# The last block's stores cut at multiples of 16 rows and dealt to three DMA queues, its second half stored first

## Chip, cores, metric

One NeuronCore of a Trainium2 chip runs the whole program. The metric is the device time of an execution in microseconds (us); lower is better. Before the change: 2807.3 us, median of three executions.

## The reference, cut to what matters

```python
def reference(**kwargs):
    X = np.fft.rfft(x, axis=1)                       # x: (8, 3008, 256)
    y = np.fft.irfft(X * (filt_r + 1j * filt_i)[None], n=3008, axis=1)
    x = y.reshape(8 * 3008, 256)
    h = x @ w_in                                     # (24064, 2048)
    g = h * np.clip(h + 3.0, 0.0, 6.0) / 6.0
    return g @ w_out                                 # (24064, 256), float32
```

## The kernel before

The filter is done by small DFT matmuls beside the two large matrix products. The products go over 47 blocks of 512 tokens, each in eight steps (376 steps). When a block's last matmul is done, DVE puts its output tile `o` together from PSUM, Pool adds a part that ACT has copied to the tile `p`, and SP stores it. (The engines: PE does the matmuls, DVE, ACT and Pool work on elements, and SP, ACT and Pool can each issue DMAs; what one of them issues is called its queue here. A DMA has landed at its last semaphore event in the trace. DRAIN is an instruction that every engine has in the program's closing line.) For all blocks but the last that happens beside the next block's matmuls. The last block has nothing beside it.

```python
N, NA, NC, TOK, BLK, P, D = 3008, 47, 64, 94, 512, 128, 256

def out_4(k):
    p5 = st["po", k][2][:, 0, :, :]
    nc.vector.tensor_tensor(out=o_at(k, 1, 1), in0=p5, in1=o_at(k, 1, 0), op=ALU.add)                     # L493
    nc.vector.tensor_tensor(out=o_at(k, 0, 1), in0=p5, in1=o_at(k, 0, 1), op=ALU.add)                     # L494
    nc.gpsimd.tensor_tensor(out=o_at(k, 1, 0), in0=st["o", k][1][:, 1, :, :], in1=o_at(k, 1, 0), op=ALU.add)  # L495

def out_5(k):
    nc.vector.tensor_tensor(out=o_at(k, 0, 1), in0=st.pop(("po", k))[3][:, 1, :, :], in1=o_at(k, 0, 1), op=ALU.add)  # L498
    o = st.pop(("o", k))[0].rearrange("p t u d -> p (t u) d")
    t, end = k * BLK, (k + 1) * BLK
    while t < end:
        b, r = divmod(t, N); j, r = divmod(r, TOK); h, a = divmod(r, NA)   # (written on one line here)
        p = t % P
        m = min(NA - a, P - p)
        nc.sync.dma_start(raw(out, b * N + a * NC + outer(j, h), [[NC * D, m], [1, D]]), o[p:p + m, t % BLK // P, :])  # L508
        t += m
# ... at the very end of the program:
out_4(NBLK - 1)
out_5(NBLK - 1)
```

Tokens lie in runs of 47 whose rows are 64 rows apart in the output, so one store carries at most 47 rows of 1 KB. Pool also issues DMAs of its own all through the body: 224 stores of `z_tmp`, 84 of `g_tmp` and 16 loads of weights, 324 in all, the last at 2196.5 us.

Of the kernel before, what the change touches and what calls it, by code (L numbers as in the profile page):

```python
# [13 lines left out]
ALU = mybir.AluOpType  # L14
# [8 lines left out]
N = 3008  # L23
NA = 47
NC = 64
KH = 24
NF = N // 2 + 1
P = 128
D = 256
# [14 lines left out]
BLK = 512  # L44
NBLK = B * N // BLK
# [4 lines left out]
def outer(j, h):  # L50

    return (NC - j if j else HC) if h else j
# [49 lines left out]
def kernel(  # L102
# [9 lines left out]
    nc = tc.nc  # L112
# [11 lines left out]
    def pool(name, bufs, **kw):  # L124
        return ctx.enter_context(tc.tile_pool(name=name, bufs=bufs, **kw))
# [13 lines left out]
    op = pool("op", 2)  # L139
# [16 lines left out]
    st = {}  # L156

    def raw(src, row, ap):
        return bass.AP(tensor=src.tensor, offset=src.offset + row * D, ap=ap)
# [184 lines left out]
    for b in range(B):  # L344
        j = 0
# [5 lines left out]
    def token(i):  # L351
        b, j, n = chunks[i]
        return b * N + j * TOK, n * TOK
# [124 lines left out]
    def o_at(k, t, d):  # L478
        return st["o", k][0][:, t, :, ts(d, P)]
# [11 lines left out]
# [5 lines that stand above are left out]

    def out_5(k):
        nc.vector.tensor_tensor(out=o_at(k, 0, 1), in0=st.pop(("po", k))[3][:, 1, :, :], in1=o_at(k, 0, 1), op=ALU.add)  # L498
        o = st.pop(("o", k))[0].rearrange("p t u d -> p (t u) d")

        t, end = k * BLK, (k + 1) * BLK
        while t < end:
            b, r = divmod(t, N)
            j, r = divmod(r, TOK)
            h, a = divmod(r, NA)
            p = t % P
            m = min(NA - a, P - p)
            nc.sync.dma_start(raw(out, b * N + a * NC + outer(j, h), [[NC * D, m], [1, D]]),  # L508
                              o[p:p + m, t % BLK // P, :])
            t += m  # L510

# [9 lines left out]
    with tc.manual_schedule():  # L521
# [77 lines left out]
        for i in range(2, len(chunks)):  # L599
            k = token(i)[0] // BLK  # L600
# [52 lines left out]
        for i in range(len(items) + 1):  # L653
            up = i < len(items)
            k, p = items[min(i, len(items) - 1)]
            dn = i > 0
            kd, pd = items[i - 1]
            def do(early):
                for fn, a in plan.get((i, early), ()):
                    fn(*a)  # L660
# [23 lines left out]
            if dn and pd == 0 and kd:  # L684
                out_5(kd - 1)
# [8 lines left out]
                if pd == NP - 1:  # L694
                    out_3(kd)
            do(False)
        out_4(NBLK - 1)
        out_5(NBLK - 1)


# [28 lines left out]
```

## Time and profile before

| | before |
|---|---|
| time, median of 3 | 2807.3 us (2805.96 to 2807.75) |
| span of the profiled execution | 2805.7 us, granted clock 0.987 |
| end of the last matmul | 2785.3 us |
| first store of the last block issued | 2787.0 us |
| tail: end of the last matmul to end of span | 20.4 us |
| Pool's closing DRAIN | 2786.3 to 2795.6 us |

The **tail** is the number to watch: only this part of the program differs between the two kernels. On each engine the instructions before it are the same and in the same order. Its pieces are in the lines that the prediction shows.

### The profile page before, as it was taken

How to read it: one execution, taken by the hardware profiler on the slowest of the kernel's cores; microseconds unless marked ns; L12 is line 12 of the kernel's file. 1: busy time of each engine (PE TensorE's matmuls, PEld its weight loads, DVE VectorE, ACT ScalarE, POOL GpSimd, SP SyncE). 2: the span in 40 equal slices, each digit the busy share in tenths (PEclk: the TensorE clock that was granted, in tenths of full speed). 3: DMA queues.
4: the chain of work that ended last, by engine and by line, in shares of the span. 5: the costliest groups of instructions: out<-in, count | busy, mean ns of one | idle time of the engine just before them, and what ended most of it. 6: DMA issues, size and time to landing. Idle time of an engine off the chain costs nothing.

```text
span 2805.7 us, 47214 instructions
## 1 busy us (share of the span) xinstructions
PE 2700.1 (96%) x18096; PEld 2395.8 (85%) x18096; DVE 1993.9 (71%) x3463; ACT 1325.9 (47%) x2672; POOL 456.4 (16%) x663
## 2 busy tenths in 40 slices
PE   3589999999999999999999999999999999999997
PEld 1269888989889998899988998899988999999996
DVE  5877875777657776577756777567775777766665
ACT  1144445454554445544455445544455444445443
POOL 6470112110120111201021101210012100000000
PEclk9699999999999999999999999999999999999998
DMA  7544223321223212222133221332123321100000
GB/s 216 175 112 118 63 55 90 90 68 43 74 72 85 80 50 71 80 73 75 51 84 89 72 56 45 86 91 70 49 56 90 97 66 42 42 25 23 17 8 16
DMA packets 121800, 200.82 MB, mean 72 GB/s; under 512 B 22280, under 2 KB 86600, under 8 KB 121448
## 3 DMA queue, kind: packets, MB, share of 16 engines
q1 hardware_dynamic: 97108, 139.48, 17.3%
q0 software_dynamic: 19776, 52.46, 8.0%
q10 hardware_dynamic: 4692, 5.88, 0.7%
q8 instruction: 143, 2.34, 0.3%
q14 instruction: 81, 0.66, 0.1%
HBM read 122.75 MB, written 74.97 MB: 70 GB/s over the span
## 4 chain that ended last, share of the span: by engine, by line
PE 92%; DVE 3%; DMA 2%; ACT 1%; issue 1%; POOL 0%; SPq 0%; ACTq 0%; POOLq 0%; DVEq 0%
PE po L468 41%; PE al L392 23%; PE be L392 17%; PE psn L367 4%; PE psf L300 3%; PE psf L275 2%; PE psf L329 2%; DMA z_tmp<-t 1%; DVE g L442 0%; DVE y L319 0%; DMA g_tmp<-t 0%; DMA xn<-in_x_dram 0%; DVE s L314 0%; DVE s L313 0%; ACT t L278 0%
## 5 line engine op out<-in xcount | busy, mean ns | idle before, releaser
L468 PEld LDWEIGHTS po<-w_out,g 128*128 128x128 f32 x10528 | 1398.3, 192 | 152.4 <-issue 37.3
L468 PE MATMUL po<-w_out,g 128*128 128x128 f32 x10528 | 1430.6, 276 | 4.9 <-DVE g L442 4.6
L442 DVE SCALAR_TENSOR_TENSOR g<-r,h 128x512 f32<-128x512 f32 x752 | 519.0, 690 | 268.9 <-ACT r L437 256.1
L437 ACT ACTIVATE r<-h,half_c 128x512 f32<-128x512 f32 x752 | 542.7, 722 | 337.3 <-DVE h L418 325.1
L392 PE MATMUL al<-xt,w_in 128*128 128x256 f32 x2256 | 675.6, 381 | 6.4 <-DVE h L423 3.3
L418 DVE TENSOR_TENSOR h<-be,s 128x512 f32<-128x512 f32 x376 | 259.8, 691 | 272.1 <-PE be L392 250.5
L392 PE MATMUL be<-xn,w_in 128*128 128x256 f32 x1504 | 447.8, 379 | 0.0
L392 PEld LDWEIGHTS al<-xt,w_in 128*128 128x128 f32 x2256 | 342.6, 192 | 10.5 <-DVE h L423 3.8
L392 PEld LDWEIGHTS be<-xn,w_in 128*128 128x128 f32 x1504 | 286.1, 190 | 38.9
L432 ACT ACTIVATE h<-al 128x256 f32<-128x256 f32 x376 | 144.4, 384 | 355.6 <-PE al L392 355.6
L423 DVE TENSOR_TENSOR h<-al,s 128x256 f32<-128x256 f32 x376 | 159.6, 425 | 167.5 <-PE al L392 166.0
L450 DVE TENSOR_TENSOR g<-g 128x512 f32<-128x512 f32 x376 | 260.2, 692 | 12.9
L413 ACT ACTIVATE s<-al 128x256 f32<-128x256 f32 x376 | 144.6, 384 | 199.4 <-PE al L392 199.4
L404 ACT ACTIVATE s<-be 128x256 f32<-128x256 f32 x376 | 144.4, 384 | 181.0 <-PE be L392 181.0
L392 PE MATMUL al<-xn,w_in 128*128 128x256 f32 x752 | 225.2, 381 | 0.5 <-ACT h L432 0.5
L392 PE MATMUL be<-xt,w_in 128*128 128x256 f32 x752 | 224.1, 380 | 0.0
L288 POOL DMA_DIRECT2D z_tmp<-t x224 | 131.5, 591 | 417.2 <-ACT t L278 407.7
L452 DVE TENSOR_TENSOR g<-g 128x256 f32<-128x256 f32 x376 | 168.8, 449 | 12.8
L403 ACT ACTIVATE s<-al 128x256 f32<-128x256 f32 x376 | 144.5, 384 | 70.2 <-PE al L392 70.2
L495 POOL TENSOR_TENSOR o<-p,o 128x256 f32<-128x256 f32 x47 | 34.1, 725 | 878.1 <-ACT t L332 361.3
L449 DVE TENSOR_TENSOR g<-g 128x256 f32<-128x256 f32 x376 | 161.9, 430 | 12.8
L392 PEld LDWEIGHTS be<-xt,w_in 128*128 128x128 f32 x752 | 143.2, 190 | 19.4
(71 smaller groups left out, 1783.7 us busy)
## 6 DMA issues: line engine op xcount, KB each, us to landing
t<-z_tmp SPq DMA_DIRECT2D x48, 512.0 KB
t<-g_tmp SPq DMA_DIRECT2D x188, 120.0 KB
z_tmp<-t POOLq DMA_DIRECT2D x224, 96.0 KB, 3.0
g_tmp<-t POOLq DMA_DIRECT2D x84, 256.0 KB, 3.8
out_dram<-o SPq DMA_DIRECT2D x328, 47.0 KB
xs<-in_x_dram SPq DMA_DIRECT2D x120, 128.0 KB
ft<-in_filt_r_dram SPq DMA_DIRECT2D x96, 128.0 KB
ft<-in_filt_i_dram SPq DMA_DIRECT2D x96, 128.0 KB
```

The lines of the kernel that those rows point to most:

```text
L392: nc.tensor.matmul(ps, w_in[p][:, w, :], x, start=start, stop=stop, skip_group_check=True)
L403: nc.scalar.activation(out=s[:, 0, :], in_=al, func=AXT.Copy)
L404: nc.scalar.activation(out=s5, in_=be[:, 1, :], func=AXT.Copy)
L413: nc.scalar.activation(out=s[:, 1, :], in_=al, func=AXT.Copy)
L418: nc.vector.tensor_tensor(out=st["h"][0].rearrange("p (a n) -> p a n", a=2), in0=be, in1=s, op=ALU.add)
L423: nc.vector.tensor_tensor(out=st["h"][1][:, 256:512], in0=al, in1=s5, op=ALU.add)
L437: nc.scalar.activation(out=r, in_=st["h"][i], func=AXT.Relu, bias=half_c, scale=1.0 / 6.0)
L442: nc.vector.scalar_tensor_tensor(out=st["g", k, p][:, o:o + 2, :].rearrange("p a n -> p (a n)"), in0=st["r", i], scalar=1.0, in1=st["h"][i ...
L449: v.tensor_tensor(out=g[:, G1, :], in0=g[:, G3, :], in1=g[:, G22, :], op=ALU.add)
L450: v.tensor_tensor(out=g[:, G3:G2 + 1:2, :], in0=g[:, G3:G1 + 1, :], in1=g[:, G11:G11 + 1, :].broadcast_to([P, 2, 256]), op=ALU.subtract)
L452: v.tensor_tensor(out=g[:, G4, :], in0=g[:, G12, :], in1=g[:, G2, :], op=ALU.subtract)
L468: nc.tensor.matmul(st["po", k][bank][:, part, u, :], g[:, a, ts(u, P)], w_out[p][:, w, :], start=(p == 0 and n in OPENS and u == 0), stop= ...
```

## The change

Its intent: the stores of 47 rows run on one DMA engine, so cut the last block's stores into pieces whose row count many engines divide; deal them to SP, ACT and Pool in turn; and finish and store the second half of the block first, so that its stores go out while DVE still works on the first half. To do so, Pool's addition of the last block moves to DVE.

```diff
     def out_5(k):
         nc.vector.tensor_tensor(out=o_at(k, 0, 1), in0=st.pop(("po", k))[3][:, 1, :, :], in1=o_at(k, 0, 1), op=ALU.add)
-        o = st.pop(("o", k))[0].rearrange("p t u d -> p (t u) d")
-        t, end = k * BLK, (k + 1) * BLK
+        store(k, 0, 4)
+
+    def store(k, u0, u1, qs=None):
+        o = st["o", k][0].rearrange("p t u d -> p (t u) d")
+        t, end, i = k * BLK + u0 * P, k * BLK + u1 * P, 0
         while t < end:
...
             m = min(NA - a, P - p)
-            nc.sync.dma_start(raw(out, ...), o[p:p + m, t % BLK // P, :])
+            if qs:
+                m = m // 16 * 16 or m
+            q = qs[i % len(qs)] if qs else nc.sync
+            i += 1
+            q.dma_start(raw(out, ...), o[p:p + m, t % BLK // P, :])
             t += m
...
-        out_4(NBLK - 1)
-        out_5(NBLK - 1)
+        k, v, add = NBLK - 1, nc.vector.tensor_tensor, ALU.add
+        po, qs = st["po", k], (nc.sync, nc.scalar, nc.gpsimd)
+        v(out=o_at(k, 1, 1), in0=po[2][:, 0, :, :], in1=o_at(k, 1, 0), op=add)              # L708
+        v(out=o_at(k, 1, 0), in0=st["o", k][1][:, 1, :, :], in1=o_at(k, 1, 0), op=add)      # L709
+        store(k, 2, 4, qs)
+        v(out=o_at(k, 0, 1), in0=po[2][:, 0, :, :], in1=o_at(k, 0, 1), op=add)              # L711
+        v(out=o_at(k, 0, 1), in0=po[3][:, 1, :, :], in1=o_at(k, 0, 1), op=add)              # L712
+        store(k, 0, 2, qs)
```

More of the change, by code (lines that the diff above doesn't have):

```diff
@@ L507, in out_5 @@
             m = min(NA - a, P - p)
-            nc.sync.dma_start(raw(out, b * N + a * NC + outer(j, h), [[NC * D, m], [1, D]]),
+            if qs:
+                m = m // 16 * 16 or m
+            q = qs[i % len(qs)] if qs else nc.sync
+            i += 1
+            q.dma_start(raw(out, b * N + a * NC + outer(j, h), [[NC * D, m], [1, D]]),
                               o[p:p + m, t % BLK // P, :])
```

## The prediction

> **What bounds the kernel now.** I read the page first, for the bound of the body. Over 2780 of the 2806 us TensorE sets the pace, and the change leaves those instructions alone. The busy line and the first lines of the costliest groups say so; the reader should note that PE is at 96% of the span and that its idle time is a few us.
>
> ```profile
> PE 2700.1 (96%) x18096; PEld 2395.8 (85%) x18096; DVE 1993.9 (71%) x3463; ACT 1325.9 (47%) x2672; POOL 456.4 (16%) x663
> L468 PE MATMUL po<-w_out,g 128*128 128x128 f32 x10528 | 1430.6, 276 | 4.9 <-DVE g L442 4.6
> ```
>
> The change touches only what follows the last matmul, so I read the timeline from there. Columns are start, duration, engine, line, operation.
>
> ```profile
> 2782.33 2.94 PE L468 MATMUL po<-w_out,g 128*128 128x128 f32 x24 [0.62 <-DVE g L442]
> ...
> 2785.31 0.43 DVE L489 TENSOR_TENSOR o<-po,o 128x256 f32<-128x256 f32 x1
> 2785.77 0.42 DVE L493 TENSOR_TENSOR o<-po,o 128x256 f32<-128x256 f32 x1
> 2786.11 0.41 DVE L494 TENSOR_TENSOR o<-po,o 128x256 f32<-128x256 f32 x1
> 2786.33 0.72 POOL L495 TENSOR_TENSOR o<-p,o 128x256 f32<-128x256 f32 x1 [44.15 <-DVE o L493]
> 2786.56 0.42 DVE L498 TENSOR_TENSOR o<-po,o 128x256 f32<-128x256 f32 x1
> 2787.01 10.44 SPq L508 DMA_DIRECT2D out_dram<-o  x14
> ```
>
> Matmuls end at 2785.3, arithmetic at 2787.05, and the span at 2805.7: a tail of 18.7 us in which only the 14 stores of the last block run. The chain that ended last does not show this tail (its last piece is Pool's at 2786.3), because nothing in it counts as busy; a reader who stops at the chain misses it. The view by windows gives the rate, in its last column in GB/s:
>
> ```profile
> 2796.00:2800.00 4.00, 0.00 (x0) 0.00 (x0) 0.00 (x0) 0.00 (x0) 0.00 (x0) 0.50 0.07 26
> 2800.00:2804.10 4.10, 0.00 (x0) 0.00 (x0) 0.00 (x0) 0.00 (x0) 0.00 (x0) 0.50 0.07 24
> 2804.10:2805.70 1.60, 0.00 (x0) 0.00 (x0) 0.00 (x0) 0.00 (x0) 0.00 (x0) 0.50 0.00 1
> ```
>
> A share of 0.07 of 16 engines is about one engine, at 24 GB/s, or 42 ns for a row of 1 KB. Last bytes at 2804.1, last landing at about 2804.5, then 1.2 us of closing waits and barrier.
>
> **What the Trainium skill says.** "DMA: Bandwidth & Descriptors", section "Why a DMA increments its semaphore by 16 and not by 1": a copy runs on the largest k up to 16 that divides its slowest dimension, on the lowest-numbered k engines. A store of 47 rows (prime) runs on one engine, and always on the same one. Seven of the 14 stores have 47 rows; the others have 42, 39, 8, 26, 21, 13, 34 rows, k = 14, 13, 8, 13, 7, 13, 2. The k sum to 77, and the DMA view of the tail agrees to the packet:
>
> ```profile
> DMA packets 589, 0.52 MB, mean 20 GB/s; under 512 B 77, under 2 KB 589, under 8 KB 589
> ```
>
> 512 rows of 1 KB and 77 small completion packets. Engine 0 carries 7 x 47 rows plus 3+3+1+2+3+1+17 = 359 rows; 359 x 42 ns = 15.1 us, and from the first bytes at about 2788.3 to 2804.1 there are 15.8 us. So the tail is one engine's queue.
>
> The same page, "Issuing engines are not separate DMA queues": issuing from several engines saves only issue time, as all share the 16 engines. No row of this trace contradicts it. "Perfetto Trace Analysis", section "DMA Instruction — HWDGE (DVE, Sync)": the recorded duration covers waiting for and using the descriptor generator, not the data. That explains stores of 0.25 to 0.4 us at first and up to 1.9 us later in the tail: they are held up behind the full engine, so the short ones are the true cost. The waits of the tail show the rest:
>
> ```profile
> SPq L724 <- DMA out_dram<-o: 6.9, 3, 3.0
> SPq L508 <- DMA out_dram<-o: 0.5, 1, 0.5
> ```
>
> The second is a store that waits for an earlier store with which it shares no data. In the trace's semaphore events the stores of SP and the DMAs of ACT take turns on eight semaphores, and the ninth waits for the first to land. Pool's DMAs have eight of their own.
>
> **The change, part by part.**
> 1. Rows. Pieces are cut to multiples of 16, so 26 stores in place of 14: 13 for each half, with k of 16, 5, 16, 15, 16, 15, 13, 16, 2, 16, 15, 16, 15 and then 16, 10, 16, 15, 16, 7, 8, 16, 15, 16, 15, 16, 10. Engine 0 gets 18 + 18 = 36 rows, 36 x 42 ns = 1.5 us in place of 15.1. The engines are no longer the bound; issue and landing are.
> 2. Arithmetic. The Pool addition (0.72 us) moves to DVE (0.42) and the order changes. L489 ends at 2785.74; first addition 2785.77 to 2786.19, second 0.34 later (the spacing of L493 to L494), done at about 2786.55. The first half's stores start at 2786.6 in place of 2787.0. Third and fourth additions end at about 2787.4, behind the first half's issue.
> 3. SP and ACT. SP has 10 stores, ACT 8. An unhindered issue takes about 0.36 us (SP's first stores in the tail start 0.30 to 0.42 apart; ACT's early stores of z_tmp have a median of 0.37). SP: 2786.6 + 9 x 0.36 = 2789.8 for its last start, plus about 0.3 for semaphores in turn, 2790.1. The first store of the tail landed 1.55 us after its issue, so the last lands at about 2791.7. ACT ends earlier.
> 4. Pool. 8 stores. Its view of z_tmp stores, four in a row, gives 582 ns each, back to back, and landing 2.5 us after issue:
>
> ```profile
> L288 POOL DMA_DIRECT2D z_tmp<-t x4: 582/582/583, 2194.8 to 2196.5; - x4
> DMA to landing us min/median/max: 2.3/2.5/2.7
> ```
>
> Start 2786.7 (Pool woke 0.13 after DVE before), last issue 2786.7 + 7 x 0.58 = 2790.8, end of issue 2791.35, landed by 2793.2. Pool is the slowest of the three queues.
> 5. The end. After the last landing 1.2 us, so 2794.4 in the span if nothing else is waited for, 11.3 us less than now.
>
> But Pool's queue has one more instruction, its closing DRAIN. Before, it was hidden under the stores:
>
> ```profile
> L724 POOLq DRAIN  x1: 9260/9260/9260, 2786.3 to 2786.3; - x1
> ```
>
> It starts with Pool's last addition, which ended at 2787.05, and ends at 2795.56: 8.5 us of its own, with no DMA of Pool's in flight (the last was issued at 2196.5). Pool's other drains in the trace, at the start before any DMA and again at the very end, take 0.17 us or less. No page of the skill that I found bears on it. My reading is bookkeeping over the 324 DMAs that Pool issued (224 + 84 + 16), 26 ns each as an estimate. The barrier at the end needs Pool. If the drain now comes after Pool's last store, it runs from 2791.35 to about 2799.9, or to 2800.6 if the full 9.26 is charged; the barrier took 0.74 us after SP's arrival at 2804.96, so the span ends at about 2801. Time is span plus 1.6 (2807.3 against 2805.7): 2802.5.
>
> **The rivals.**
> (a) The drain decides: about 2802.5, a gain of 5. For it: the drain is there, on an engine that the change gives more to do[...]. Against it: its end before came 60 ns after a landing of a 47-row store, so it may have been waiting for something of the stores; and it may overlap Pool's issue if the queue runs ahead. I give this 60%.
> (b) The drain is short or overlapped, the last landing of Pool's stores decides: 2794.4 + 1.6 = 2796, a gain of 11. 33%.
> (c) The additions of the second half wait until the first half's stores have been read, as they write the same tile. That adds some 2 us to the second half, 2798 without the drain. Against it: L498 wrote the tile while Pool's L495 was still working in it, so parts of the tile are tracked apart. 5%.
> (d) Small rows over 16 engines move slower than one engine's 24 GB/s each. Early in the kernel the page shows 216 GB/s; at that rate 0.52 MB takes 2.4 us, still under the 4.6 us of Pool's issue. It hides.
>
> **Range and chances.** (a) gives 2801 to 2804, (b) 2795 to 2797, with 0.9 us of run to run spread on either side. Weighting 60 to 40, I set 2801.5 with a range of 2795 to 2803.5. Two per cent is 56 us and the whole tail is 18.7, so faster by over 2% is impossible by this account; slower by over 2% would need a second mechanism in the body, where no instruction changes.
>
> **What would show each step.** Small packets in the tail rise from 77 to about 380 (249 from SP and ACT, and 16 for each of Pool's 8), and no window of the tail runs at 24 GB/s for long. SP stores of 1.9 us disappear. Pool shows 8 stores 0.58 apart ending near 2791.3. Last bytes come before 2793. Pool's DRAIN then tells (a) from (b): at 8 us or more, ending near 2800, it is (a); under 2 us it is (b). The prediction is wrong if the tail is still 15 us, if the stores of the second half start later than 2789, or if the matmuls end elsewhere than at 2785.3.

## The result, and the profile after

Correct. Six executions of each kernel: after, median 2804.57 us (2801.06 to 2806.39); before, median 2807.48 us (2805.05 to 2810.26). Ratio 0.9988, 95% interval 0.9976 to 1.0001: the same within 2%, as foreseen, but 1.07 us above the upper end of my range. Ratios here are the mean time of one kernel's fast executions over that of the other's of the same rounds, so not quite the ratio of the medians quoted.

In the profiled execution (2801.94 us, span 2800.2, clock 0.988) the last matmul ends at 2784.44, and the tail is 15.7 us in place of 20.4. Its timeline (start, duration, engine, line, operation) answers to the one in the prediction:

```profile
2784.48 0.42 DVE L489 TENSOR_TENSOR o<-po,o 128x256 f32<-128x256 f32 x1
2784.94 0.42 DVE L708 TENSOR_TENSOR o<-po,o 128x256 f32<-128x256 f32 x1
2785.40 0.42 DVE L709 TENSOR_TENSOR o<-p,o 128x256 f32<-128x256 f32 x1
2785.74 0.42 DVE L711 TENSOR_TENSOR o<-po,o 128x256 f32<-128x256 f32 x1
2785.85 4.46 SPq L516 DMA_DIRECT2D out_dram<-o  x10
2785.85 3.65 ACTq L516 DMA_DIRECT2D out_dram<-o  x8
2786.11 4.12 POOL L516 DMA_DIRECT2D out_dram<-o  x8 [44.77 <-DVE o L709]
2786.19 0.42 DVE L712 TENSOR_TENSOR o<-po,o 128x256 f32<-128x256 f32 x1
```

All 26 stores are issued within 4.5 us, where the 14 of before took 10.4. The view by windows (from:to, length, busy time of PE, PEld, DVE, ACT and POOL, granted clock, DMA share, GB/s) shows that the data follows closely behind:

```profile
2787.00:2789.00 2.00, 0.00 (x0) 0.00 (x0) 0.00 (x0) 0.00 (x0) 2.00 (x5) 0.50 0.53 127
2789.00:2791.00 2.00, 0.00 (x0) 0.00 (x0) 0.00 (x0) 0.00 (x0) 1.24 (x3) 0.50 0.49 125
2791.00:2793.00 2.00, 0.00 (x0) 0.00 (x0) 0.00 (x0) 0.00 (x0) 0.00 (x0) 0.50 0.00 0
2793.00:2795.00 2.00, 0.00 (x0) 0.00 (x0) 0.00 (x0) 0.00 (x0) 0.00 (x0) 0.50 0.00 0
```

About 126 GB/s for four us, half of the 16 engines' time, and no data to speak of after 2791. The last landing in the trace's semaphore events is at 2792.5. But the span ends at 2800.2. What fills the 7.6 us between is in the list of the closing line's instructions and in SP's waits (engine, line, waited for: us in total, times, longest):

```profile
L739 POOLq DRAIN  x1: 10133/10133/10133, 2789.2 to 2789.2; - x1
```

```profile
SPq L739 <- PEq L739: 7.3, 2, 6.8
SPq L739 <- DMA out_dram<-o: 1.8, 2, 1.2
```

Pool's DRAIN runs from 2789.25 to 2799.38, and 0.78 us later the program ends. The wait of 6.8 us is put down to PE, but PE's own closing drain was over at 2784.5: SP stands at a barrier, of which Pool is the last to arrive. A wait for several engines is put down to one of them, and here it is the wrong one; the DRAIN row tells who it was.

So the stores now end 11.1 us earlier from the last matmul (8.1 in place of 19.2), and the program ends only 4.7 us earlier. Pool's drain, hidden under the stores before, now comes after Pool's last store and takes 9.1 us from the end of that store's issue.

### The profile page after: what moved, and what is told of

Its sections match the earlier page's. It is cut to its first block, busy times and chain, and to the rows that moved or that the text cites. A ratio compares the mean times of both kernels' runs of the same rounds, so it can differ in the third digit from the quotient of the medians.

```text
span 2800.2 us, 47225 instructions
## 1 busy us (share of the span) xinstructions
PE 2699.6 (96%) x18096; PEld 2397.0 (86%) x18096; DVE 1994.4 (71%) x3464; ACT 1324.2 (47%) x2672; POOL 459.9 (16%) x670
## 3 DMA queue, kind: packets, MB, share of 16 engines
q10 hardware_dynamic: 4974, 6.05, 0.8%
## 4 chain that ended last, share of the span: by engine, by line
PE 92%; DVE 3%; DMA 2%; POOL 1%; ACT 1%; issue 1%; SPq 0%; ACTq 0%; POOLq 0%; DVEq 0%
PE po L468 42%; PE al L392 23%; PE be L392 17%; PE psn L367 4%; PE psf L300 3%; PE psf L275 2%; PE psf L329 2%; DMA z_tmp<-t 1%; DMA xn<-in_x_dram 1%; DVE y L319 0%; DMA g_tmp<-t 0%; DVE s L314 0%; DVE s L313 0%; DVE g L442 0%; ACT t L278 0%
```

## Experiments

Ten kernel runs, eight on one chip; order_alone and rows_two_queues ran on another, with the kernel before timed beside them there. I compare tails, because they repeat closely (the changed kernel gave 15.72 us in both of its traces, while its last matmul ended at 2784.44 and 2785.85), and give the timed ratio where there is one. "+x" is us after the end of the last matmul.

| kernel | first store | last issue ends | last landing | Pool's drain ends | tail | ratio to before (95%) |
|---|---|---|---|---|---|---|
| before | +1.74 | +12.18 | +19.20 | +10.29 | 20.42 | 1 |
| order_alone | +1.41 | +13.65 | +19.08 | long before | 20.30 | not timed |
| queues_alone | +1.74 | +4.63 | +14.02 | +14.19 | 15.05 | not timed |
| rows_alone | +1.74 | +12.26 | +13.33 | +10.29 | 14.30 | 0.9981 (0.9965 to 0.9996) |
| rows_two_queues | +1.74 | +7.32 | +8.49 | +10.29 | 11.07 | 0.9964 (0.9948 to 0.9981) |
| two_queues | +1.41 | +7.27 | +8.26 | long before | 9.22 | 0.9959 (0.9947 to 0.9972) |
| after (ratio: after_again) | +1.41 | +5.87 | +8.10 | +14.95 | 15.72 | 0.9984 (0.9972 to 0.9997) |
| early_drain | +1.41 | +5.87 | +8.09 | +8.26 | 9.07 | 0.9962 (0.9949 to 0.9974) |
| more_pool_dmas | +1.41 | +8.62 | +9.77 | +10.28 | 11.06 | 0.9972 (0.9958 to 0.9985) |
| pool_12_late | +1.41 | +5.84 | +8.07 | +15.90 | 16.68 | not timed |
| pool_60_late | +1.41 | +5.85 | +8.06 | +9.95 | 10.73 | 0.9968 (0.9952 to 0.9983) |

**after_again**: no edit, five rounds.

> The changed kernel once more, with five rounds beside the kernel before, to part two readings of the miss (2804.6 measured, 2801.5 predicted). Reading N: the tail gain is what the traces show (20.4 us from last matmul to end before, 15.8 after, so 4.6), and single executions differ by up to 5 us with the granted TensorE clock (the three runs at 0.988 to 0.989 took 2801.1 to 2804.1, the three at 0.981 to 0.982 took 2805.0 to 2806.4). It expects a ratio of 0.9983 and, at equal clock, runs of before 4 to 6 us longer. Reading T: in unprofiled or later executions the closing drain of Pool is longer, so the gain is really 2 to 3 us: ratio 0.9990 and a gain of under 3.5 us at equal clock.

Measured: median 2803.35 us (2801.56 to 2804.93) against 2807.26 for before (2805.47 to 2809.17), ratio 0.9984; drain 10.137 us, tail 15.72. That is the size that reading N gave, but the interval holds T's 0.9990 as well. What speaks against T is this second trace: drain and tail are those of the first. The part of N that blames the clock is not shown: an execution at 0.983 took 2801.56 and one at 0.982 took 2804.93, and before, 2805.47 at 0.988 and 2808.27 at 0.987.

**two_queues**: take Pool out of the stores.

```diff
-        po, qs = st["po", k], (nc.sync, nc.scalar, nc.gpsimd)
+        po, qs = st["po", k], (nc.sync, nc.scalar)
```

> The changed kernel with its last stores on SP and ACT only. Pool then has nothing to do after the block before, so its drain is over long before the end. Theory D (Pool's closing drain sets the end after the change): the end follows the last landing; 13 stores each on SP and ACT at about 0.42 us, held a little by the eight semaphores, last issue near 2791.5, landing near 2793.3, span 2794.5 on the same body, about 5.5 us under the changed kernel, ratio to before 0.9962. Rival L (landing and barrier set the end, the drain only fills the wait): no gain over the changed kernel, rather 1 us of loss as 26 stores go over two queues.

Measured: median 2795.69 us, tail 9.22. From its timeline and its closing line's instructions:

```profile
2788.63 5.86 SPq L516 DMA_DIRECT2D out_dram<-o  x14
2788.63 5.22 ACTq L516 DMA_DIRECT2D out_dram<-o  x12
```

```profile
L739 POOLq DRAIN  x1: 9267/9267/9267, 2743.4 to 2743.4; - x1
```

The drain costs its 9.27 us in the middle of the last block, where nobody waits for Pool, and the end follows the last landing by 0.96 us. Rival L falls: with one queue fewer and the issue ending 1.4 us later, the tail is 6.5 us shorter than the changed kernel's (5.5 was expected).

**early_drain**: keep all three queues and let Pool drain once while the last block still computes.

```diff
             do(False)
+            if i == len(items) - 6:
+                nc.gpsimd.drain()
```

> The changed kernel with one more drain of Pool in the middle of the last block, where Pool is idle for some 40 us. Theory C (the drain walks through the DMAs that Pool issued since its last drain, some 27 ns each): the early drain takes about 8.5 us unseen, the closing one under 3 us (8 DMAs and the last landing), span 2793.5 on the same body, 6.5 us under the changed kernel, ratio to before 0.9960. Rival F (a drain at the end costs a fixed 8.5 us or so): the closing drain stays at 9 to 10 us and the time stays that of the changed kernel.

Measured: median 2797.02 us, tail 9.07. The early drain, and the closing one (which overlaps Pool's last stores):

```profile
L706 POOLq DRAIN  x1: 9267/9267/9267, 2743.9 to 2743.9; - x1
```

```profile
L741 POOLq DRAIN  x1: 3436/3436/3436, 2792.6 to 2792.6; - x1
```

The closing drain ends 0.17 us after the last landing. A second drain with few DMAs issued since the first is short, so the cost is not a fixed one of the program's end: rival F falls.

**more_pool_dmas**: 160 more small DMAs of Pool in the body.

```diff
+    s_d = nc.dram_tensor("s_tmp", (160, 16, P), FP32, kind="Internal").ap()
...
             do(False)
+            if i % 2 == 0 and 40 <= i < 360:
+                nc.gpsimd.dma_start(s_d[i // 2 - 20], wa[0:16, :])
```

> The changed kernel with 160 more small DMAs of Pool (8 KB each, from a constant tile to a scratch tensor that nobody reads) spread over the body, where Pool is 16% busy. Theory C: the closing drain grows by 160 x 27 ns = 4.3 us, to about 14.4 us, and the time by 4.3. Rival F: drain unchanged near 10.1 us and time unchanged within 1 us.

Measured: the opposite. The closing drain shrank to 2.26 us, the tail to 11.06, and the kernel, doing more, was faster than the change. My count of 324 at 27 ns each fell with it, and so did the fixed cost. The timeline of Pool in its tail has the clue:

```profile
2787.62 2.08 POOL L518 DMA_DIRECT2D out_dram<-o  x4 [44.78 <-DVE o L713]
2792.36 1.02 POOL L518 DMA_DIRECT2D out_dram<-o  x2 [2.66 <-issue]
2793.54 1.02 POOL L518 DMA_DIRECT2D out_dram<-o  x2 [0.16 <-issue]
```

Pool paused 2.66 us in the midst of its stores for nothing that the profile shows ("issue"). In the whole trace such pauses come before Pool's 126th, 247th, 368th and 489th DMA: every 121. In the traces of before and after, a pause of 2.7 us stands before the 229th. Whatever Pool does there, only three of this kernel's 492 DMAs came after the 489th, and its drain was short. That gave theory R: Pool clears its record of issued DMAs about every 121, and the drain works through those issued since. The clearing is a guess; no record shows it.

**pool_12_late** and **pool_60_late**: 12 or 60 more small Pool DMAs, late in the body, to set the number left over.

```diff
             do(False)
+            if 350 <= i < 362:              # the other: 310 <= i < 370
+                nc.gpsimd.dma_start(s_d[i - 350], wa[0:16, :])
```

> The changed kernel with 12 more small Pool DMAs at steps 350 to 361 of 376, so that Pool's last DMAs before the tail are recent. The traces so far: in the kernel before and after Pool paused 2.7 us before its 229th DMA, in the run with 160 more it paused at the 126th, 247th, 368th and 489th and its closing drain was short. Theory R: Pool clears its record of issued DMAs about every 121, and the drain walks what has been issued since, about 89 ns each (8.51 us for 95 before, 9.15 for 103 after). Then 115 are left: 10.2 us of its own after the last store's issue, the tail about 16.8 us, one more than after. Rival A: recent Pool DMAs make the drain short, whatever the number (tail about 11 us). Rival W: the drain walks all DMAs since the start at 27 ns, which the run with 160 more already speaks against: tail 16.1 us.

> The changed kernel with 60 more small Pool DMAs at steps 310 to 369 of 376. Theory R: the clearing falls at about the 350th DMA, in the body where it costs nothing, and 332 + 60 - 350 = 42 are left for the closing drain, 3.7 us of its own after the last store's issue (against 9.2 after the change), so the tail is about 10.5 us, 5.3 less than after, and the time about 2798.5. Rival A (recent DMAs): tail about 11 us as well, but with a drain that ends with the last landing and not after it. Rival F (fixed drain): tail 15.8.

Measured: tails of 16.68 and 10.73 us. The closing drains, of pool_12_late and then of pool_60_late:

```profile
L743 POOLq DRAIN  x1: 11117/11117/11117, 2791.3 to 2791.3; - x1
```

```profile
L743 POOLq DRAIN  x1: 5166/5166/5166, 2789.3 to 2789.3; - x1
```

And from Pool's timeline of pool_60_late, at its 350th DMA, 121 after the 229th:

```profile
2526.76 1.00 POOL L708 DMA_DIRECT2D s_tmp<-wa  x2 [1.85 <-issue]
```

Both tails came within 0.25 us of theory R (16.8 and 10.5), and the pause came where it was expected. Counted from the end of Pool's last instruction before the drain: 4.20 us with 42 DMAs left, 8.51 with 95 (before), 9.14 with 103 (after) and 10.13 with 115. (The DMA that the pause stands before is not counted; with it each number is one higher.) From 42 to 115 that is 5.93 us over 73 DMAs, 81 ns each, with some 0.8 us besides. Rival A falls: 12 recent DMAs made the drain longer, not shorter.

Three runs lie above this line: early_drain's closing drain took 2.45 us for 8 DMAs (the line gives 1.4), more_pool_dmas's 1.66 for 3 (1.0), and queues_alone's 9.56 for 100 (8.9). So the number is not all that counts. In these three, Pool has stores in the tail and the line would have ended before the last landing of the tail; the drain ended 0.17, 0.51 and 0.17 us after that landing. It looks as if it waited for the stores, but no run was made to test that.

**rows_alone**: before, with the row cut only.

```diff
             m = min(NA - a, P - p)
+            if k == NBLK - 1:
+                m = m // 16 * 16 or m
```

> The kernel before with one part of the change: the last block's stores cut into multiples of 16 rows (26 stores), still all on SP, after all the arithmetic in its old place. I measure the tail, from the end of the last matmul to the end of the span: 20.4 us before, 15.8 after the change. Theory: the one engine's queue was the cost, and issue replaces it: first store 1.7 us after the last matmul, 26 x 0.42 = 10.9 us of issue, 2 us to land, 1.0 for the closing waits: tail 15.6 us, with Pool's drain hidden (over some 10.3 us after the last matmul). So rows alone would give as much as the whole change, ratio 0.9983. Rival: without the two other queues the row cut gives little, tail over 18 us.

Measured: median 2802.18 us, ratio 0.9981, tail 14.30, better than expected by 1.3 and better than the whole change by 1.4 (the timed ratios, 0.9981 and 0.9984, cannot tell these two apart). SP's line of the timeline:

```profile
2787.39 10.52 SPq L510 DMA_DIRECT2D out_dram<-o  x26
```

The issue took the 10.5 us expected; the last, small store landed 1.07 us after its issue ended, sooner than the 2 us I allowed. Now SP's issue is the bound, and Pool's drain ends at +10.29, hidden.

**queues_alone**: before, with whole rows dealt to three queues.

```diff
+        qs = (nc.sync, nc.scalar, nc.gpsimd) if k == NBLK - 1 else (nc.sync,)
...
-            nc.sync.dma_start(raw(out, ...), ...)
+            i += 1
+            qs[i % len(qs)].dma_start(raw(out, ...), ...)
```

> The kernel before with another part alone: the last block's 14 stores whole, dealt to ACT, Pool and SP in turn, old arithmetic. Four of the seven stores of 47 rows are then on SP and ACT and so on engine 0: 188 rows plus some 20 of others, 9 us from about 3 us after the last matmul, end near 13.5 us. Pool's last store is issued some 4.5 us after the last matmul and its drain, if it takes 8.9 us of its own from there, ends at 13.4, the span at 14.2 us. Theory D expects a closing drain of 8.5 to 10 us that starts after Pool's stores and a tail of about 14.2 us. If Pool's stores too sit on one engine, the tail is over 16 us.

Measured: one execution, 2800.34 us, tail 15.05, 0.85 more than expected. From its windows and its closing line's instructions:

```profile
2792.00:2794.00 2.00, 0.00 (x0) 0.00 (x0) 0.00 (x0) 0.00 (x0) 0.00 (x0) 0.50 0.07 24
```

```profile
L726 POOLq DRAIN  x1: 10381/10381/10381, 2787.3 to 2787.3; - x1
```

It runs at 24 GB/s from 2792 to 2796, one engine again, and the last landing (+14.02, a store of ACT's) and the end of the drain (+14.19) fall nearly together. The drain was longer than the 8.5 to 10 us expected. So this run does not part the two, beyond showing that whole rows over three queues still queue on one engine.

**order_alone**: the change's order and arithmetic, with whole rows on SP.

```diff
             if qs:
-                m = m // 16 * 16 or m
+                pass
...
-        po, qs = st["po", k], (nc.sync, nc.scalar, nc.gpsimd)
+        po, qs = st["po", k], (nc.sync,)
```

> The third part alone: the changed kernel's arithmetic and its storing of the second half first, but whole rows and all on SP. Engine 0 still gets 359 rows at 42 ns, 15.1 us; the first store comes 1.41 us after the last matmul instead of 1.74, and Pool has no arithmetic in the tail. Tail by the theory 20.42 - 0.33 = 20.1 us. Rival: the order is worth more than the earlier start, tail under 19 us.

Measured: one execution, 2809.1 us, tail 20.30. The order with the additions on DVE gives 0.12 us by itself.

**rows_two_queues**: before's arithmetic (Pool's addition still in the tail), cut rows, SP and ACT.

```diff
+            if k == NBLK - 1:
+                m = m // 16 * 16 or m
...
+        qs = (nc.sync, nc.scalar) if k == NBLK - 1 else (nc.sync,)
```

> The kernel before with cut rows and two queues (SP and ACT), but the old arithmetic, so that Pool's addition (L495) is still in the tail and its closing drain starts only then. Stores: first at +1.74 us from the last matmul, 13 on each queue, last landing near +8.6. In the kernel before the drain ended at +10.29. Theory D: the drain, not the landing, sets the end: tail 10.29 + 0.77 = 11.05 us, 1.8 more than the same stores with the addition moved to DVE (9.22), ratio to before 0.9966. Rival: the drain is only long beside slow stores or beside Pool's own stores, so the landing decides: tail 9.6 us.

Measured: ratio 0.9964, tail 11.07, where theory D gave 11.05. The drain is the one of before:

```profile
L728 POOLq DRAIN  x1: 9262/9262/9262, 2785.5 to 2785.5; - x1
```

The last landing is at +8.49, the drain ends at +10.29. So the new order with Pool's addition moved to DVE, which looked like a matter of 0.3 us, is worth 1.85 us (11.07 to 9.22), of which the earlier landing explains 0.23: the move takes the drain out of the tail. The traces show this; the timed ratios of the two runs (0.9964 and 0.9959) overlap.

**The parts together**, added in this order (in another order the shares differ: order_alone gave 0.12). Cutting rows: 20.42 to 14.30. ACT as a second queue: to 11.07. Additions on DVE, second half first: to 9.22. Pool as a third queue: back up to 15.72. Three parts of the change gained 11.2 us and the fourth gave 6.5 back.

## Why the prediction was right or wrong

1. **One engine's queue is the tail: right.** Before, 77 small packets. (The first bytes left at 2787.8, not 2788.3 as the prediction reads; one engine's 15.1 us then stand in 16.3.) After, SP (q1) and ACT (q10) moved 328 + 282 = 610 packets, which is what their 361 rows and my 249 small ones add up to. The cut alone took 6.1 us off.

```profile
DMA packets 866, 0.53 MB, mean 24 GB/s; under 512 B 402, under 2 KB 818, under 8 KB 866
q0 software_dynamic: 256, 0.16, 3.3%
q1 hardware_dynamic: 328, 0.19, 3.3%
q10 hardware_dynamic: 282, 0.18, 3.2%
```

The sum is 402 small ones rather than 380: Pool's 8 stores (q0) made 153, not 128. The 25 more are as many as the engines that got no row of a store: 1, 14, 9 and 1 for its stores of 15, 2, 7 and 15 rows.
2. **Arithmetic: right.** The first store 1.41 us after the last matmul in place of 1.74; I had 0.4 us earlier, it was 0.33.
3. **SP and ACT: too short by 1.7 us.** The last start came 4.1 us after the first (I had 3.5), and the last store landed 2.6 us after its issue, where I had taken the 1.55 of the first store of the old tail. Last landing at +8.1, not +6.4.
4. **Pool: right in sum.** 0.52 us for a store in place of 0.58; last landing at +7.9 as predicted. It was not clearly the slowest queue: in this trace SP landed last, by 0.2 us, and in after_again Pool did, by 0.2 us.
5. **Rival (a), the drain decides: right.** Predicted tail 2801 - 2785.3 = 15.7 us, measured 15.72. So close a hit is partly luck: Pool's issue ended at +5.8 where +6.05 was predicted, and the drain took 9.1 us from there, between the 8.5 and 9.26 that the prediction left open. Its cause was not right. "My reading is bookkeeping over the 324 DMAs that Pool issued (224 + 84 + 16), 26 ns each" failed: 160 more made the drain shorter. What counts is the number issued since Pool's last pause, 81 ns each, and in three runs something besides, which stays open. The end of the old drain 60 ns after a landing was chance: at +10.29 it ended in rows_alone and rows_two_queues too, where the landings fall elsewhere.
6. **The range: the step that made the prediction wrong.** It read "with 0.9 us of run to run spread on either side. Weighting 60 to 40, I set 2801.5 with a range of 2795 to 2803.5." Two things failed in it. One is the spread: 0.9 us came from three executions. The later six of before ran from 2805.05 to 2810.26, and in twelve traces the last matmul ended between 2783.47 and 2787.80, though what runs before it is the same but for the extra Pool DMAs of three of them and the early drain of one. The other is the upper end: account (a) gave 2801 to 2804, so 2804.9 with the 0.9 on top, which holds the measured 2804.57. Mixing it with (b), which did not happen, drew the end down to 2803.5, below (a)'s own. (The sum is off too: 60 to 40 of 2802.5 and 2796 is 2799.9, not 2801.5.) With the spread that the runs showed, 2.6 us to each side, (a)'s middle of 2802.5 alone reaches past 2805. Of eleven executions of the changed kernel five fell in the range; they lie from 2801.06 to 2806.39.

   Nor does the tail hide a second effect. Over the seven timed kernels other than before, the timed gain (one minus the ratio, times before's mean) and the tail's gain agree within 1.5 us: 4.5 and 4.7 for after_again, 5.3 and 6.1 for rows_alone, 11.5 and 11.2 for two_queues. The first measurement of the change gave 3.4 against 4.7, and its interval holds both. Why the body itself varies by some 4 us from one execution to the next stays open; the mean clock does not order the executions.

Not settled: what Pool does in its pauses, and why the first fell elsewhere in the kernel before (a late start at the 109th DMA may be one) than in the run with 160 more.

## What to carry to other kernels

At the end of a program look past the chain of busy work: the landing of the stores, the barrier and all but 0.5 to 0.8 us of Pool's closing drain were not in it here, and an engine that is off the path in the body can be the last to arrive. A queue that is free to issue is not free to finish: here Pool's queue saved SP and ACT 1.4 us of issue, brought the last landing forward by 0.16 us (8.26 to 8.10), and cost 6.5 us of tail through its drain. Either keep late DMAs off it (two_queues, 2795.7 us, the simplest of the versions that beat both kernels) or drain it early where it idles, and count rows so that a store divides among many engines.

## What the Trainium skill lacked or had wrong

- No page that I found has the cost of a DRAIN on GpSimd after many DMAs of its own; it belongs on "GPSIMD Engine Reference" or on "DMA: Bandwidth & Descriptors". These runs: 4.2 us with 42 issued since the last pause, 10.1 us with 115, 81 ns each; longer than that by 0.6 to 1.0 us in the three runs where it would have ended before the last landing.
- No page that I found has the pauses of Pool's DMA issue: 1.85 to 2.71 us in these traces, in two of the kernels 121 of its DMAs apart.
- "DMA: Bandwidth & Descriptors", section "Issuing engines are not separate DMA queues", says that issuing from several engines saves only issue time, "which is usually small relative to the DMA itself". The first half agrees. For 26 stores of up to 32 KB in a row the second does not: 26 stores took 10.5 us to issue from one queue, of 11.6 from the first issue to the last landing, and a second queue took 3.2 us off the tail.
- The same page's rule for the number of engines of a transfer, in "Why a DMA increments its semaphore by 16 and not by 1", held to the packet on SP and ACT (77 small packets before, 249 after). That all 16 engines post for a store from GpSimd gives 128 for 8 stores; 153 packets under 512 B were counted. What the page lacks is the other 25, as many as the engines without a row of a store; queues_alone has 88 from Pool in place of 80, and 8 engines without a row.
